# Attention's outputs turned as 4-byte words, and a rearranged start, in a fused attention and MLP kernel

## The chip, the cores and the metric

The kernel runs on one core of a Trainium2 chip. The metric is the device time of one execution in microseconds (us), lower is better. Five engines work side by side, each with its own queue of instructions: PE multiplies matrices (its weight loads are shown apart as PEld), DVE does vector work, ACT evaluates functions and copies, POOL copies, clears and issues DMAs, and SP issues DMAs. Data comes and goes by 16 DMA engines.

## The reference

Local and global attention for 8 batches and 8 heads of 64 dimensions, 512 local and 32 global tokens, and then an MLP with a gated activation over all 4,352 tokens.

```python
s_g = scale * matmul(q_g, k_all^T); out_g = softmax(s_g) @ v_all     # 32 global tokens see all 544
s_ll = where(|i - j| <= 32, scale * matmul(q_l, k_l^T), -1e9)        # 512 local tokens: a band
s_l = concat([scale * matmul(q_l, k_g^T), s_ll])                     # and the 32 global ones
out_l = softmax(s_l) @ concat([v_g, v_l])
x = concat([out_g, out_l]).transpose(0, 2, 1, 3).reshape(4352, 512)
h = x @ w_in                                                         # 512 -> 2048
out = (h * clip(h + 3, 0, 6) / 6) @ w_out                            # 2048 -> 512
```

## The kernel before, in words

**Stages of a batch.** q and k come with tokens on the partitions and are turned by DVE in 32x32 blocks (`turn_words` for batches 0 and 1, in 4-byte words that hold two dimensions of one token; `turn_wide` for the rest). Scores (PE, L712 and L699) go to PSUM. L743 adds the mask and takes the extreme on DVE, L749 is the exponential on ACT, L758 turns the weights of attention on PE, L318 copies them out, L776 sums the values on PE. `normal` divides by the sums (reciprocal L785, product L786) and `xturn` (L799) turns the result on DVE from tokens-by-dimensions to dimensions-by-tokens, into the tile `xt` with four chunks of 128 dimensions. The 32 global tokens go the same way: scores L824 (batches 0 and 1) and L816, value sums L857, product L874, turn L877 into `xg`.

**The MLP.** `first` (L899) multiplies one 128-column tile of w_in with the four chunks of `xt` (L907, 512 columns a matmul; batch 0 comes in parts of 128, 128 and 256 columns), then L918 (relu on ACT, PSUM to `t1`) and L914 (the gate on DVE, to `gts`). `second` (L934) sums 16 chunks of `gts` with w_out, and the result is copied to `ot` and stored. The global tokens of all batches pass through `first` and `second` at the very end.

**The two dimensions of a word.** In `turn_words` q and k are read as words, so that a partition holds two dimensions of each token side by side. The scores of batches 0 and 1 therefore run in two rounds (`bb` 0 and 1), each of which streams every second value (`pairs(kt)[rows, c, ..., bb]`).

**The order of the work.** Every operation is an `Op` with a planned cost per engine, its dependencies and the buffers that it takes, in one of some 35 named streams with a rank each. `Plan.lay` (L122) walks through planned time, and at each step lays the ready operation with the lowest rank on its engine; where an operation may run on several engines, the one that ends it first gets it (DVE with a surcharge `SPARE`). The result is one fixed order per engine. On the chip an engine works through its order and waits for what its data need, whatever the plan thought of the time. The stream names that matter here: `l0` (POOL's loads of the start), `g0` (SP's staging loads of batch 0's q and k), `ga` (ACT's loads of global k and q), `sh` (SP's), `gc`, `gd`, `gp` (casts of global k and q), `msk` (masks), `kg` (halo copies of k, L612), `vs` (strips of v, L542), `tq` (turns of q and k), `nm` and `xp` (`normal` and `xturn`), `t1` and `gate` (L918 and L914).

**The start.** SP loads half of batch 0's q and k as fp32 into the room of w_in (four loads, cast by L431). POOL draws a band for the masks (L385), then issues the other halves of q and k (cast by the DMA), v_g, four pieces of v, four of w_in. `ident` (masks.py) and `clear` (L369, zeroes and ones in the second buffers of `vg`, `kt`, `v0` and `vs`) stand in POOL's order between the first and the second piece of w_in. Batch 1's q follows (to the room of `xt`), k, v, and w_out. `once` (L466) loads global q or k of batch 0 or 1 to 32 partitions in one DMA, and four casts of 32 partitions (L478 on ACT, L480 on DVE or POOL) spread it to four quarters.

Of the kernel before, what the change touches and what calls it, by code (L numbers as in the profile page):

```python
# [37 lines left out]
class Plan:  # L38
# [7 lines left out]
    SPARE, PHASES = 0.5, 9  # L46
# [146 lines left out]
def kernel(  # L193
# [64 lines left out]
    graw0 = tiles("graw0_", 1, [W, 2, H, D], FP32)[0]  # L258
# [37 lines left out]
    for name, rank in (("l0", 0), ("ld", 5), ("lq", -2), ("sh", 0), ("sq", 0), ("st", 3.5), ("g0", 0), ("ga", -9), ("first", -9), ("pad", -30), ("gc", -6), ("gd", 3), ("gp", 3.9), ("cast", -5), ("msk", lambda n: 1 if n < 9 else 1.25), ("tq", lambda n: 0 if n < 8 else 3), ("kg", 0.5), ("vs", 1.5), ("clr", 1),  # L296
                       ("s", 0.5), ("mx", lambda n: 1.2 if n < 33 else 2.7), ("ex", 1.9), ("t", -0.5), ("etc", 0), ("av", -0.7), ("nm", 0.7),
                       ("xp", -0.5), ("gx", 1),
                       ("mf", lambda n: 9 + n * 1e-3), ("ms", lambda n: 9 + (n + len(PARTS) * NDFF + 2) * 1e-3), ("t1", 0), ("gate", -0.7), ("ot", 3)):
        plan.stream(name, rank)  # L300
    for name in ("l0", "ld", "lq", "sh", "st", "g0", "ga", "sq"):
        plan.stream("dq" + name, 0 if name in ("l0", "ld", "lq") else -1)
# [47 lines left out]

    def half(r):

        return slice(r * D, (r + 1) * D)
# [5 lines left out]
    def setup():  # L359
        nc.vector.memset(mxs[0], 0.0)  # L360
        clear(nc.vector, 0)
# [7 lines left out]
    def clear(eng, r):  # L369
        eng.memset(vg[r], 0.0)  # L370
        eng.memset(vg[r][0:W, :, D:D1], 1.0)
        for e in range(2):
# [43 lines left out]

    def stage_loads():
# [3 lines left out]
        there = [[load("g0", "SP", 0.47, 0.65, stage[:, i, c, :], raw(src, 0)[:, c, :], lat=(2.6, 3.1, 3.2, 5.7)[2 * c + i]) for i, src in enumerate((q_l, k_l))]  # L421
# [15 lines left out]
        lower = plan.add("l0", Op(("POOL", 1.9), band))  # L437
        for i, src in enumerate((q_l, k_l)):
            st["qk"][1, i] = [load("l0", "POOL", 0.75, 1.6, nat(0, i)[:, NC // 2:, :], raw(src, 0)[:, NC // 2:, :], lat=4.2 - 0.4 * i)]
        vg_load(0, "l0")  # L440
        for m in (2, 3, NU, 1, 0, NU + 1):
            made["mask", m] = [plan.add("msk", Op(("ACT", 0.21), lambda o=o, i=i: nc.scalar.copy(out=o, in_=i), [lower])) for o, i in places(m)]
# [23 lines left out]
    def once(b, k, src, name):  # L466

        raw_ = (graw0[:, k] if b else ots[k][0:W].rearrange("g (h d) -> g h d", d=D))
        got = load("sh" if b else "ga", "SP" if b else "ACT", 0.47, 0.45 if b else 0.3, raw_, src[b].rearrange("h g d -> g h d"), [w_in_l[1][1]] if b else ())
        g = Buf("gn" + name, 1)  # L470
        state[b]["gn", k] = g
        state[b]["gl"][k] = []
        for e in range(2):
            for f in range(2):
                def cast(engine, e=e, f=f):
                    o, i = gn0[k][quarter(e, f)], raw_.rearrange("g (c e) d -> g e c d", e=2)[:, e]
                    if engine == "ACT":
                        nc.scalar.copy(out=o, in_=i)  # L478
                    else:
                        (nc.gpsimd if engine == "POOL" else nc.vector).tensor_copy(out=o, in_=i)  # L480
                op = Op({"POOL": 0.43, "ACT": 0.42} if b else {"ACT": 0.42, "DVE": 0.4} if k else {"ACT": 0.42}, None, [got], [] if e or f else [g])
                op.emit = lambda op=op, cast=cast: cast(op.engine)
                state[b]["gl"][k].append(plan.add("gp" if b else "gc" if k else "gd", op))
# [33 lines left out]
    def v_loads(b, to):  # L517
# [4 lines left out]
        if b == 0:  # L522
            made["ident"] = plan.add("clr", Op(("POOL", 0.55), lambda: make_identity(nc, ident)))
        vl = [load(to, "POOL", 0.88, 1.05 if b else 1.25, lambda j=j: v0[v.slot][:, j, :, 0:D],
                   v_l[b, :, j * P:(j + 1) * P, :].rearrange("h s d -> s h d"), lat=LATE[b] if b else 3.3 - 0.4 * j) for j in range(NJ)]
# [58 lines left out]
    def turn_words(b, st, k):  # L584
# [23 lines left out]
        def halo(c0, c1, e, engine):  # L608
            copy = nc.scalar.copy if engine == "ACT" else nc.gpsimd.tensor_copy
# [5 lines left out]
        for q in range(n):  # L615
# [10 lines left out]
            else:  # L626
                st["k"].append(plan.add("tq", Op(("DVE", 1.9 / n), lambda c0=c0, c1=c1: turn_q(c0, c1), st["qk"][q, 0],
                                                 [] if b == 0 else [k])))
                a = plan.add("tq", Op(("DVE", 1.95 / n), lambda c0=c0, c1=c1: turn_k(c0, c1), st["qk"][q, 1]))
                st["k"].append(a)  # L630
            for e in range(2):
                h = Op({"POOL": 0.55, "ACT": 0.5}, None, [a])
# [45 lines left out]
    def local(b, n, spare, halves=False):  # L678
# [103 lines left out]
        def normal():  # L782
# [3 lines left out]
            nc.vector.tensor_tensor(out=xs[x.slot].rearrange("p g (a d) -> p g a d", a=2), in0=o[:, :, 0:D].rearrange("p g (d a) -> p g a d", a=2),  # L786
                                    in1=r.rearrange("p g (a d) -> p g a d", a=1).to_broadcast([P, 2 * NC, 2, W]), op=ALU.mult)
# [9 lines left out]
        def xturn():  # L797

            nc.vector.transpose(out=xts[xt.slot][:, :, n * P:(n + 1) * P].rearrange("p k (t q) -> p t k q", q=W),  # L799
                                in_=xs[x.slot].rearrange("p (t k) (a q) -> p t (k a) q", k=2, a=2))  # L800
        st["xT", n] = plan.add("xp", Op(("DVE", 0.7), xturn, done, new, [x]))
# [60 lines left out]
    def globe_values(b):  # L862
# [7 lines left out]
        def normal():  # L870
# [3 lines left out]
            nc.vector.tensor_tensor(out=xgns[xgn.slot].rearrange("p k (a d) -> p k a d", a=2), in0=o[:, :, 0:D].rearrange("p k (d a) -> p k a d", a=2),  # L874
                                    in1=r.rearrange("p k (a d) -> p k a d", a=1).to_broadcast([P, 2, 2, W]), op=ALU.mult)
        n = plan.add("nm", Op(("DVE", 0.45), normal, [a], [rec, xgn], [av, rec]))
        st["xg"] = plan.add("gx", Op(("DVE", 0.22), lambda: nc.vector.transpose(  # L877
            out=xg[:, :, b * Sg:(b + 1) * Sg], in_=xgns[xgn.slot].rearrange("p k (a q) -> p (k a) q", q=W)), [n], (), [xgn]))
# [73 lines left out]
    def moe_first(b):  # L952
# [4 lines left out]
        for at, part in enumerate(PARTS if b == 0 else [range(NJ)]):  # L957
# [3 lines left out]
            for c in range(0, NDFF, per):  # L961
# [6 lines left out]
                got = first(lambda m, cols=cols: xts[xt.slot][:, m, cols], n, cs, gated,  # L968
# [10 lines left out]
    def moe_global():  # L979
        gd, gb = {}, {}  # L980
        deps = [state[b]["xg"] for b in range(B)]
        for c in range(0, NDFF, 2):
# [3 lines left out]
            gd[c] = gd[c + 1] = first(lambda m: xg[:, m, :], B * Sg, range(c, c + 2),  # L986
# [7 lines left out]
    with tc.manual_schedule():  # L994
        clean = plan.add("first", Op(("DVE", 0.1), lambda: nc.vector.memset(zero, 0.0)))
        plan.add("pad", Op(("PE", 4.0), lambda: [nc.tensor.matmul(out=aps[0][0:W, 0, 0:2], lhsT=zero, rhs=zero[:, 0:2], start=True, stop=True) for _ in range(100)], [clean],
# [6 lines left out]
        made["clear"] = plan.add("clr", Op(("POOL", 2.4), lambda: clear(nc.gpsimd, 1), [made["ident"]]))  # L1003
# [76 lines left out]
```

## Time and profile before

| | |
|---|---|
| median of 3 runs | 327.26 us (326.31 to 327.92) |
| profiled execution | 328.56 us, of which the span from the first to the last instruction is 326.8 us |
| granted PE clock | 0.999 |
| L934, second layer, 560 matmuls | 130.8 us busy |
| L907, first layer, 704 matmuls | 121.0 us (640 on `xt`) and 8.9 us (64 on `xg`) |
| L914, gate | 92.1 us on DVE |
| L749, exponential | 84.9 us on ACT |
| L786, product | 32 of 692 ns on DVE |
| L799, turn | 32 of 704 ns on DVE |
| L877, global turn | 8 of 288 ns on DVE |
| L478 and L480, casts of global q and k | 10 of some 400 ns on ACT, 4 of 411 on POOL, 2 of 331 on DVE |

The profile shows one execution. Section 2 of its page cuts the span into 40 slices of 8.17 us, and each digit is the tenths of the slice in which an engine was busy. The chain follows the work back from the last instruction. A row of the windows gives the length of a stretch and each engine's busy time in it, then the PE clock, the DMA engines' mean busy share (over 1 where packets of several queues lie on top of each other) and GB/s. A row of the timeline has start, length, engine, line, operation, output and input, and in brackets how long the engine was idle before it and what ended that. Groups have a count, busy time, mean ns of one and idle time before.

### The profile page before, as it was taken

What the parts mean: (1) busy time and instruction counts of PE and PEld (TensorE: products, weight loads), DVE (VectorE), ACT (ScalarE), POOL (GpSimd) and SP (SyncE); (2) the same over time, 40 slices, a digit from 0 to 9 for tenths busy, and PEclk for the clock granted to TensorE, in tenths of its full rate; (3) what the DMA queues carried; (4) which work ended last, traced back from release to release, by engine and by line L of the source; (5) the groups of instructions that cost most, each with busy time, mean ns of one, the idle gap of its engine ahead of it and who ended that gap; (6) DMA issues with size and microseconds to landing.
All of it is one profiled execution on the core that took longest, in us unless ns stands there. A gap on an engine that the chain in (4) does not pass through costs nothing.

```text
span 326.8 us, 11215 instructions
## 1 busy us (share of the span) xinstructions
PE 305.8 (94%) x4484; PEld 172.8 (53%) x4484; DVE 258.4 (79%) x913; ACT 238.3 (73%) x550; POOL 157.7 (48%) x205
## 2 busy tenths in 40 slices
PE   4477898799999999999999999999999999999995
PEld 4356784454555545555555555555455545556654
DVE  7788996789989897989998999889989985742210
ACT  7999678557895788868876997699759965643221
POOL 9999999029955935665009944963900000000000
PEclk9999999999999999999999999999999999999999
DMA  8999999959952995199949993999111012011223
GB/s 201 180 215 190 188 212 170 230 152 178 200 85 66 140 184 138 46 111 160 217 118 99 226 138 48 148 157 174 33 35 34 2 34 67 0 34 32 65 53 79
DMA packets 104821, 39.54 MB, mean 121 GB/s; under 512 B 91648, under 2 KB 97536, under 8 KB 104768
## 3 DMA queue, kind: packets, MB, share of 16 engines
q0 software_dynamic: 91392, 16.91, 63.9%
q1 hardware_dynamic: 12832, 21.78, 26.8%
q8 instruction: 35, 0.57, 0.7%
q10 hardware_dynamic: 544, 0.13, 0.2%
q14 instruction: 18, 0.15, 0.2%
HBM read 35.13 MB, written 8.91 MB: 135 GB/s over the span
## 4 chain that ended last, share of the span: by engine, by line
PE 86%; POOL 5%; DMA 3%; DVE 2%; issue 2%; ACT 0%; POOLq 0%
PE m L934 37%; PE m L907 35%; PE t L758 4%; DMA xt<-in_q_l_dram 3%; PE a L776 3%; PE s L699 3%; PE t L847 1%; POOL vs L542 1%; PE s L816 1%; POOL v L308 1%; PE a L857 1%; PE s L712 1%; POOL win L308 1%; DVE qt L590 1%; DVE kt L595 1%
## 5 line engine op out<-in xcount | busy, mean ns | idle before, releaser
L934 PE MATMUL m<-wout,gts 128*128 128x512 f16 (+1 forms) x560 | 130.8, 373 | 1.8 <-issue 1.8
L907 PE MATMUL m<-xt,win 128*128 128x512 f16 (+2 forms) x640 | 121.0, 338 | 2.2 <-DVE gts L914 1.2
L914 DVE SCALAR_TENSOR_TENSOR gts<-t,m 128x512 f16<-128x512 f32 x136 | 92.1, 682 | 34.4 <-ACT t L918 33.1
L918 ACT ACTIVATE t<-m 128x512 f32<-128x512 f32 x136 | 81.2, 597 | 34.5 <-PE m L907 31.4
L907 PEld LDWEIGHTS <-win 128*128 128x128 f16 x704 | 70.4, 114 | 48.0 <-issue 3.8
L542 POOL COPY vs<-v 32x1056 f32<-32x1056 f32 (+4 forms) x91 | 81.7, 898 | 29.1 <-DMA v<-in_v_l_dram 24.8
L749 ACT ACTIVATE ex<-sm,mx 128x128 f16<-128x128 f32 x256 | 84.9, 394 | 7.2 <-DVE mx L743 6.5
L934 PEld LDWEIGHTS <-gts 128*128 128x128 f16 x560 | 51.6, 98 | 52.1 <-issue 3.5
L743 DVE CUSTOM_DVE_ANT_0 sm<-s,mask 128x128 f32<-128x128 f32 x240 | 56.2, 285 | 7.2 <-PE s L712 4.1
L308 POOL DMA_DIRECT2D rawq<-in_q_l_dram x12 | 12.6, 1059 | 46.3 <-DVE rec L785 24.3
L318 ACT COPY et<-t 128x1024 f16<-128x1024 f16 x28 | 28.1, 1005 | 8.1 <-PE t L758 8.0
L308 POOL DMA_DIRECT2D v<-in_v_l_dram x32 | 28.2, 896 | 0.0
L942 ACT COPY ot<-m 128x512 f32<-128x512 f32 (+1 forms) x29 | 16.5, 570 | 15.3 <-PE m L934 15.2
L786 DVE TENSOR_TENSOR x<-a,rec 128x512 f16<-128x512 f32 x32 | 22.1, 692 | 1.1
L799 DVE STREAM_TRANSPOSE xt<-x 128x512 f16<-128x512 f16 x32 | 22.5, 704 | 0.1
L758 PEld LDWEIGHTS <-ex 128*128 128x128 f16 x256 | 17.3, 101 | 9.0 <-ACT ex L749 2.7
L743 DVE DVE_READ_ACCUMULATOR2_ANT mx<- 128x1 f32 x256 | 21.3, 83 | 0.0
L758 PE MATMUL t<-ident,ex 128*128 128x128 f16 x240 | 19.9, 225 | 1.5 <-ACT ex L749 1.5
L318 ACT COPY etg<-t 128x640 f16<-128x640 f16 x16 | 11.1, 692 | 10.5 <-PE t L847 10.5
L776 PEld LDWEIGHTS <-et 128*32 128x32 f16 x1024 | 10.0, 98 | 13.1 <-ACT ex L749 4.7
L646 DVE STREAM_TRANSPOSE qt<-rawq 128x512 f16<-128x512 f16 x24 | 15.5, 680 | 0.0
L650 DVE STREAM_TRANSPOSE kt<-rawk 128x512 f16<-128x512 f16 x24 | 15.5, 679 | 0.0
(92 smaller groups left out, 221.5 us busy)
## 6 DMA issues: line engine op xcount, KB each, us to landing
out_dram<-ot SPq DMA_DIRECT2D x62, 128.0 KB, 2.9
vs<-vg SPq DMA_DIRECT2D x32, 132.0 KB, 5.4
v<-in_v_l_dram POOLq DMA_DIRECT2D x32, 128.0 KB, 6.4
rawq<-in_q_l_dram POOLq DMA_DIRECT2D x12, 256.0 KB, 5.8
rawk<-in_k_l_dram POOLq DMA_DIRECT2D x12, 256.0 KB, 6.8
rawq<-rawq SPq DMA_DIRECT2D x12, 254.0 KB, 5.3
rawk<-rawk SPq DMA_DIRECT2D x12, 254.0 KB, 4.9
win<-in_moe_w_in_dram POOLq DMA_DIRECT2D x4, 512.0 KB, 11.3
```

The costliest lines, as they stand in the source:

```text
L308: eng.dma_start(out=o() if callable(o) else o, in_=i() if callable(i) else i)
L318: nc.scalar.copy(out=o(), in_=i())
L542: (nc.gpsimd if op.engine == "POOL" else nc.vector).tensor_copy(out=o(), in_=i())
L743: nc.vector.tensor_tensor_reduce(out=sms[sm.slot], in0=scored(c // 2)[:, z:z + P], in1=mask(m), scale=-scale, scalar=3.0e38, op0=ALU.add, ...
L749: nc.scalar.activation(out=exs[ex.slot][:, un, c, :], in_=sms[sm.slot], func=EXP, scale=-1.0, bias=mxs[mx.slot])
L758: nc.tensor.matmul(out=turned(tp)[:, z:z + P], lhsT=exs[ex.slot][:, un, c, :], rhs=ident, is_transpose=True)
L786: nc.vector.tensor_tensor(out=xs[x.slot].rearrange("p g (a d) -> p g a d", a=2), in0=o[:, :, 0:D].rearrange("p g (d a) -> p g a d", a=2), ...
L799: nc.vector.transpose(out=xts[xt.slot][:, :, n * P:(n + 1) * P].rearrange("p k (t q) -> p t k q", q=W), in_=xs[x.slot].rearrange("p (t k) ...
L907: nc.tensor.matmul(out=mps[ps.slot][:, k * n:(k + 1) * n], lhsT=column_tile(c)[:, m], rhs=x, start=(m == 0), stop=(m == KC - 1))
L914: nc.vector.scalar_tensor_tensor(out=g, in0=shape(t1s[t1.slot][:, 0:all_]), scalar=1.0, in1=shape(mps[ps.slot][:, 0:all_]), op0=ALU.min, o ...
L918: r = plan.add("t1", Op(("ACT", 0.09 + all_ * 0.00083), lambda: nc.scalar.activation(out=t1s[t1.slot][:, 0:all_], in_=mps[ps.slot][:, 0:al ...
L934: nc.tensor.matmul(out=mps[ps.slot][:, 0:n], lhsT=gfn(c), rhs=w_out_t[c // 4][:, c % 4, cols], start=(c == 0), stop=(c == NDFF - 1))
```

## The change

It has five pieces.

1. `normal` writes its product in the order of the dimensions, and `xturn` and the global turn L877 move words of two dimensions, in blocks of 32 words. A partition of `xt` or `xg` then holds two dimensions of a token side by side (`dims`), and L907 streams every second value of it.
2. Global q and k of batches 0 and 1 are loaded straight to the four quarters of 128 partitions, by four DMAs each (batch 0: two of k's by ACT, the other six by SP behind the staging loads; batch 1: eight by SP), and each is cast by one operation on all partitions.
3. POOL's order at the start: band, `ident`, the clear of `vg`, the half loads of q and k, the rest of the clear, v_g, v, w_in. `clear` is cut in two for this.
4. Mask copies may go to DVE as well as ACT, and batch 0's halo copies to DVE as well as POOL and ACT. The turns of batch 1's q and k are four operations each instead of one.
5. Ranks, planned costs and planned landing times of the plan are changed, and with them the order.

The diff, cut to its core:

```diff
-    SPARE, PHASES = 0.5, 9
+    SPARE, PHASES = 0.6, 9
-    graw0 = tiles("graw0_", 1, [W, 2, H, D], FP32)[0]
+    graw0 = tiles("graw0_", 1, [P, 2, NC, D], FP32)[0]
...
-    ("st", 3.5), ... ("tq", lambda n: 0 if n < 8 else 3), ("vs", 1.5), ("nm", 0.7), ("xp", -0.5), ("t1", 0), ("gate", -0.7), ("ot", 3)
+    ("st", 2), ... ("gq", 0.1), ("tq", lambda n: 0.7 if n < 8 else 3.7), ("vs", 3.7), ("nm", 0), ("xp", 1), ("t1", -0.7), ("gate", -1.4), ("ot", 1.5)
...
+    def dims(t):
+        return t.rearrange("p (k a) s -> p k (a s)", a=2).rearrange("p k (s a) -> p k s a", a=2)
...
+    def mask_part(o, i, lower):
+        op = Op({"ACT": 0.18, "DVE": 0.11}, None, [lower])
...
         lower = plan.add("l0", Op(("POOL", 1.9), band))
+        made["ident"] = plan.add("l0", Op(("POOL", 0.55), lambda: make_identity(nc, ident)))
+        plan.add("l0", Op(("POOL", 0.62), lambda: clear_globals(nc.gpsimd, 1)))
         for i, src in enumerate((q_l, k_l)):
-            st["qk"][1, i] = [load("l0", "POOL", 0.75, 1.6, nat(0, i)[:, NC // 2:, :], raw(src, 0)[:, NC // 2:, :], lat=4.2 - 0.4 * i)]
+            st["qk"][1, i] = [load("l0", "POOL", 0.75, 1.6, nat(0, i)[:, NC // 2:, :], raw(src, 0)[:, NC // 2:, :], lat=2.1 - 0.4 * i)]
+        made["clear"] = plan.add("l0", Op(("POOL", 1.9), lambda: clear_rest(nc.gpsimd, 1)))
         vg_load(0, "l0")
...
-        got = load("sh" if b else "ga", "SP" if b else "ACT", 0.47, 0.45 if b else 0.3, raw_, src[b].rearrange("h g d -> g h d"), ...)
-        for e in range(2):
-            for f in range(2):
-                    o, i = gn0[k][quarter(e, f)], raw_.rearrange("g (c e) d -> g e c d", e=2)[:, e]
+        rows = src[b].rearrange("(c e) g d -> e g c d", e=2)
+        for f in range(2):
+            to, engine = ("sh", "SP") if b else ("ga", "ACT") if k and not f else ("gq", "SP")
+            got += [load(to, engine, 0.47, 0.15, raw_[quarter(e, f)], rows[e], ...) for e in range(2)]
+        op = Op({"POOL": 0.43, "ACT": 0.42} if b else {"ACT": 0.42, "DVE": 0.33}, None, got, [g])      # one cast, gn0[k] <- raw_
...
+                pieces = [(c0, c1)] if b == 0 else [(c, c + 1) for c in range(c0, c1)]
+                for x, y in pieces: ... turn_q(x, y)
+                for x, y in pieces: ... turn_k(x, y)
-                h = Op({"POOL": 0.55, "ACT": 0.5}, None, [a])
+                h = Op({"POOL": 0.6, "ACT": 0.5, "DVE": 0.36} if b == 0 else {"POOL": 0.6, "ACT": 0.5}, None, [a])
...
-            nc.vector.tensor_tensor(out=xs[x.slot].rearrange("p g (a d) -> p g a d", a=2), in0=o[:, :, 0:D].rearrange("p g (d a) -> p g a d", a=2), ...)
+            nc.vector.tensor_tensor(out=xs[x.slot], in0=o[:, :, 0:D], in1=r.to_broadcast([P, 2 * NC, D]), op=ALU.mult)
...
-            nc.vector.transpose(out=xts[xt.slot][:, :, n * P:(n + 1) * P].rearrange("p k (t q) -> p t k q", q=W),
-                                in_=xs[x.slot].rearrange("p (t k) (a q) -> p t (k a) q", k=2, a=2))
+            nc.vector.transpose(out=dims(xts[xt.slot])[:, :, n * P:(n + 1) * P, :].rearrange("p k s a -> p k (s a)").bitcast(FP32).rearrange("p k (t q) -> p t k q", q=W),
+                                in_=xs[x.slot].bitcast(FP32).rearrange("p (t k) q -> p t k q", k=2))
...
-                got = first(lambda m, cols=cols: xts[xt.slot][:, m, cols], n, cs, gated,
+                got = first(lambda m, cols=cols: dims(xts[xt.slot])[:, m // 2, cols, m % 2], n, cs, gated,
-            gd[c] = gd[c + 1] = first(lambda m: xg[:, m, :], B * Sg, range(c, c + 2),
+            gd[c] = gd[c + 1] = first(lambda m: dims(xg)[:, m // 2, :, m % 2], B * Sg, range(c, c + 2),
...
-        plan.add("pad", Op(("PE", 4.0), ...))
+        plan.add("pad", Op(("PE", 1.45), ...))
-        made["clear"] = plan.add("clr", Op(("POOL", 2.4), lambda: clear(nc.gpsimd, 1), [made["ident"]]))
```

More of the change, by code (lines that the diff above doesn't have):

```diff
@@ L521, in v_loads @@
         v, strips = st["v"], st["vs"]
[L522 to L525, printed above, removed]
+        vl = [load(to, "POOL", 0.88, 1.05, lambda j=j: v0[v.slot][:, j, :, 0:D],
+                   v_l[b, :, j * P:(j + 1) * P, :].rearrange("h s d -> s h d"), lat=LATE[b] if b else 1.8) for j in range(NJ)]
         def shift(u, z, n, src, js, dj, need):
@@ L608, in halo @@
         def halo(c0, c1, e, engine):
-            copy = nc.scalar.copy if engine == "ACT" else nc.gpsimd.tensor_copy
+            copy = {"ACT": nc.scalar.copy, "POOL": nc.gpsimd.tensor_copy, "DVE": nc.vector.tensor_copy}[engine]
             line = flat(kt[k.slot])
```

70 lines of the change are left out of this document (36 added, 34 removed).

## The prediction

> **What bounds the kernel now.** I read the page first: the busy shares, the 40 slices and the chain.
>
> ```profile
> PE 305.8 (94%) x4484; PEld 172.8 (53%) x4484; DVE 258.4 (79%) x913; ACT 238.3 (73%) x550; POOL 157.7 (48%) x205
> PE   4477898799999999999999999999999999999995
> DVE  7788996789989897989998999889989985742210
> DMA  8999999959952995199949993999111012011223
> PE 86%; POOL 5%; DMA 3%; DVE 2%; issue 2%; ACT 0%; POOLq 0%
> ```
>
> PE is full from the tenth slice on (some 75 us). Before that the slices are not full, and there DMA stands at 9. So the kernel is a start that ends at about 75 us, a PE-bound body, and a tail. The windows put sizes on this.
>
> ```profile
> core 0: us, PE busy (x) PEld busy (x) DVE busy (x) ACT busy (x) POOL busy (x), PEclk, DMA share, GB/s
> 0.00:24.00 24.00, 12.81 (x427) 9.86 (x428) 18.05 (x99) 21.27 (x66) 22.01 (x53) 1.00 1.23 198
> 24.00:50.00 26.00, 22.89 (x509) 19.71 (x507) 24.60 (x75) 21.15 (x50) 24.28 (x34) 1.00 1.45 196
> 50.00:75.00 25.00, 22.23 (x435) 11.64 (x434) 18.74 (x66) 15.87 (x37) 10.42 (x13) 1.00 1.43 180
> 75.00:312.00 237.00, 237.00 (x3054) 125.18 (x3052) 196.20 (x675) 177.24 (x396) 101.02 (x108) 1.00 0.81 102
> ```
>
> In each row: length of the stretch, then PE, PEld, DVE, ACT and POOL busy. Three readings. From 75 to 312 us PE has no idle time, so a faster DVE is worth nothing there. From 24 to 75 us PE idles 3.11 + 2.77 = 5.9 us. Ahead of 24 us ACT (21.27 of 24) and POOL (22.01) are the busy engines, from 24 to 50 us DVE (24.60 of 26). The clock is 1.00 throughout and needs no more thought. Then the timeline, for what starts and holds PE in that stretch.
>
> ```profile
> 8.17 0.70 POOL L308 DMA_DIRECT2D win<-in_moe_w_in_dram  x1
> 12.61 2.14 POOL L308 DMA_DIRECT2D win<-in_moe_w_in_dram  x3
> 24.01 0.47 PEld L907 LDWEIGHTS <-win 128*128 128x128 f16 x4
> 31.08 2.08 DVE L590 STREAM_TRANSPOSE qt<-xt 128x1024 f32<-128x1024 f32 x1
> 37.75 4.69 PE L907 MATMUL m<-xt,win 128*128 128x128 f16 x56 [1.22 <-DVE gts L914]
> 59.09 1.25 PE L934 MATMUL m<-wout,gts 128*128 128x512 f16 x5 [1.85 <-issue]
> ```
>
> The second piece of the first weights is issued at 12.61 us and lands 10.2 us later, at 22.8; the first layer's first matmul is at 24.0. At 31.08 batch 1's q is turned in one block of 2.08 us, and the gates behind it (L914) hold PE: 1.22 us before 37.75. The 1.85 us at 59.09 has no releaser in the profile.
>
> **The change, part by part.**
>
> (1) Word transposes. 32 transposes L799 of 512 half words (704 ns) become 32 of 256 words, 8 of L877 (288 ns) become 8 of 64 words. Word transposes are in the trace:
>
> ```profile
> L799 DVE STREAM_TRANSPOSE xt<-x 128x512 f16<-128x512 f16 x32 | 22.5, 704 | 0.1
> L590 DVE STREAM_TRANSPOSE qt<-xt 128x1024 f32<-128x1024 f32 x1 | 2.1, 2075 | 0.1
> L595 DVE STREAM_TRANSPOSE kt<-wout 128x256 f32<-128x256 f32 x4 | 2.4, 626 | 1.3 <-ACT wout L431 1.2
> L601 DVE STREAM_TRANSPOSE qg<-gn 128x128 f32<-128x128 f32 x2 | 0.6, 302 | 0.3 <-ACT gn L478 0.3
> ```
>
> 128 words take 302 ns and 96 words (L605) 239 ns, so 1.97 ns a word; 256 words come to 302 + 128 x 1.97 = 554 ns, or 626 by L595, whose outputs are scattered. I take 554, since the new outputs lie in runs of 32 words as L601's do: 0.08 to 0.15 us saved each, 2.5 to 4.8 us of DVE in all, and by the same slope 8 x 0.11 = 0.9 us for L877. [...] Of the saving, 24 turns lie beyond 75 us, under a full PE: nothing. Eight lie before, five of them from 24 to 62 us: some 0.6 us.
>
> (2) The normalisation L786 (692 ns) reads the sums in order instead of every second one. The nearest row that reads 512 sums in order is L914's gate with 682 ns: 0 to 0.01 us each, nothing.
>
> (3) The first layer streams every second value: 704 matmuls with 278,528 columns, at 216 ns per 512 in the trace. The scores of batches 0 and 1 stream every second value already. By the starts of single matmuls, eight of L712 (128 columns each) follow each other every 57 ns; contiguous L699's every 55, L907's own 128-column ones every 56. That is 0 to 2 ns per 128 columns, or 0 to 4.4 us over 2,176 such pieces. The other neighbours are the global scores, two rounds of 288 columns: 0.45 us strided (L824) against 0.43 contiguous (L816), by single ends 22 ns per 576 columns, which would be 10.6 us. No row shows a gain, because the contiguous stream is already at its pace. L824 and L712 also load twice the weights for it, which alone can make the difference, so I take 0. [...]
>
> (4) Globals to the quarters. Batch 0 drops six ACT casts (402 ns, L478) and two DVE casts (331 ns) for one whole cast each of q and k; the new one has the same 256 elements per partition, so 0.33 to 0.40 us. ACT saves 1.6 to 2.4 us ahead of 24 us. Batch 1 drops four ACT casts (400) and four POOL ones (411) for two: ACT saves 0.8 to 1.6 us near 30 us. Masks (14 copies, 214 ns) and halo copies may now go to DVE, which has 1.1 to 1.3 us idle in each 5 us from 5 to 20 us. The loads become eight instead of two per batch. Batch 0's six on SP follow the four staging loads (issue 0.4 us each) and end near 5.3 us; SP's next issue is at 10.45. Batch 1's eight take some 4 us of SP, with the next issue at 33.96, so they are covered. What is late next: k's cast now waits for a load issued at 2.6 to 3.5 us, where it was 0.73. ACT's pair landed 3.5 and 4.2 us after issue, so 6.1 to 7.7 us against the first cast at 5.29: up to 2 us later for the first scores (6.78), which the lighter ACT queue gives back by 24 us.
>
> (5) Clearing ahead of loads. On POOL's queue ident (0.5 us) and the clear of vg (0.64) now precede the two half loads (2.52 us), and the rest of the clear (10.07 to 12.66, 2.6 us) precedes vg and the four v loads (4.07). So the half loads go 1.2 us later, v 3.7 later (near 8.4 to 12.0), the first weights at 12.0 instead of 8.17. The other three follow at once and end at 14.9, where they ended at 14.75. The DMA share is 1.23 up to 24 us, so transfer time and not issue set the 22.8. The new order leaves the engines short for about 1.1 us ahead of v and starts POOL's queue 1.2 us late, partly under the staging loads. I take 1.5 us later for the weights and all behind them; bounds 0 (staging gets the engines alone, and fills the gap) and 2.7 (by the packets in the trace, 478 KB of weights are moved by 15 us, at 180 KB/us).
>
> (6) Ranks. The gate (-0.7 to -1.4), the relu (0 to -0.7) and the normalisation (0.7 to 0) go ahead of the turns (0 to 0.7), and batch 1's block of 2.08 us becomes four pieces. This is what acts on the 24 to 50 us stretch: of its 3.1 us of idle I take 2.3 to go. Of the 2.8 us in 50:75, most of it "issue", 1 goes. Planned costs and the changed masks only change the order.
>
> The sum, at the point where PE stays full: -2.3 - 1.0 for idle time, -0.6 for shorter turns, -0.4 for lighter queues ahead of 24 us (more is useless while weights are awaited), +1.5 for the weights: -2.8 us. The profiled execution took 328.56 us (span 326.8 and 1.76 around it), 1.3 over the median 327.26. From 328.56 the sum gives 325.8; on the median's side it is **324.5**. A step of 0.5%, 1.64 us, is what a measurement can tell from none: faster is below 325.6, slower above 328.9.
>
> **Rivals.**
>
> *Weights come later and eat the gain.* For it: DMA is at 9 in nearly every slice up to 65 us, so idle engines are not made up. Against it: the weights' issue ends at the same time. With 2.7 us for 1.5, and 1.5 less idle removed: -2.8 + 1.2 + 1.5, 327.2.
>
> *The strided stream is slower* (the slower side). Place: L907's stream, on the PE-bound path to the end. Price: at L824's pace 10.6 us, 324.5 + 10.6 = 335.1. It makes the kernel slower by over 0.5% from (2.8 + 1.64) / 2,176 = 2.0 ns per 128 columns, 224 ns per 512. For it: L824 against L816. Against it: L712, within 2 ns of the contiguous ones.
>
> *All the idle goes.* If the weights land no later and gates never hold PE, all 5.9 us go: 321.4. Against it: the "issue" gaps belong to no engine that the change speeds up.
>
> *It does not do what it says:* word turns at 0.63 us save half, and the sum is 324.9, inside the forecast.
>
> **Numbers.** Forecast 0.50 (own range 322.5 to 325.6). Weights later 0.25 (326 to 329.5: 0.20 within 0.5%, 0.05 slower). Strided stream 0.10, slower. All idle gone 0.13, faster. Some other lost order 0.02, slower. Faster 0.63, same 0.20, slower 0.17. The range goes from 321.0 to 329.5, which leaves out the strided stream's price, the lost order and a little of each end.
>
> **What would show it.** [...] L907 in 512 columns at 216 ns from start to start; over 221 the gain is gone. The second win piece landing at 24 to 24.5 us. No long transpose block near 31 us and PE's idle time in 24:75 below 3 us. PE still full from 75 to 312 us. I am wrong if the first layer's first matmul is after 26 us, or if PE's body changes its length by more than 2 us.

## The result and the profile after

The changed kernel takes 336.56 us (median of 4 runs, 335.01 to 336.95) against 327.58 (326.31 to 327.92) beside it: ratio 1.0273, 95% interval 1.0229 to 1.0316. It is 9.0 us slower, where 2.8 us less were forecast, and above the range.

The page of the changed kernel, its first lines and its chain of waits (its lines L922, L949, L929, L815, L803, L793 are the L907, L934, L914, L799, L786, L776 of before, with a shift of up to two lines in kernels made from it):

```profile
PE 314.4 (94%) x4484; PEld 176.1 (53%) x4484; DVE 250.8 (75%) x921; ACT 236.7 (71%) x539; POOL 154.9 (46%) x199
PE   3657799999999999999999999999999999999995
DVE  6897696788978798988996998779988855442210
DMA  7999999999962995399739949990111021111222
PE 85%; DMA 8%; DVE 3%; SPq 1%; ACT 1%; issue 0%; ACTq 0%
```

DVE works 7.6 us less and PE 8.6 us more, with the same 4,484 matmuls. In the chain POOL is gone, and DMA has grown from 3 to 8%. The same windows as before, in the changed kernel:

```profile
0.00:24.00 24.00, 12.58 (x420) 9.16 (x420) 19.16 (x97) 16.77 (x49) 21.97 (x52) 1.00 1.14 181
24.00:50.00 26.00, 21.50 (x425) 19.11 (x414) 21.40 (x69) 15.62 (x34) 15.87 (x24) 1.00 1.33 206
50.00:75.00 25.00, 24.63 (x523) 14.37 (x521) 19.32 (x82) 20.69 (x51) 13.92 (x15) 1.00 1.52 169
75.00:312.00 237.00, 236.97 (x3019) 121.96 (x3018) 188.19 (x673) 178.18 (x397) 103.10 (x111) 1.00 0.84 104
```

PE's idle time from 24 to 50 us rose from 3.11 to 4.50, that from 50 to 75 us fell from 2.77 to 0.37, and from 75 to 312 PE is as full as it was: yet it gets through 3,019 matmuls there instead of 3,054. A full engine that gets through less points to a slower engine, which no wait shows; the experiments on the stream test it. ACT is relieved ahead of 24 us (21.27 to 16.77), but the first layer starts no earlier for it. PE's timeline in the changed kernel, where the first layer begins:

```profile
19.97 0.41 PE L793 MATMUL a<-vs,et 128*32 128x65 f16 x16
22.40 0.41 PE L793 MATMUL a<-vs,et 128*32 128x65 f16 x16 [2.02 <-DMA vs<-vg]
24.70 0.41 PE L793 MATMUL a<-vs,et 128*32 128x65 f16 x16 [0.42 <-DVE x L803]
25.87 0.41 PE L793 MATMUL a<-vs,et 128*32 128x65 f16 x16 [0.76 <-DMA vs<-vg]
27.04 2.34 PE L922 MATMUL m<-xt,win 128*128 128x128 f16 x20
42.22 5.03 PE L922 MATMUL m<-xt,win 128*128 128x128 f16 x56 [1.18 <-DVE gts L929]
```

The first layer starts at 27.04 instead of 24.11, and what it waited for is not the weights, but the value sums L793 ahead of it, which wait for the strips of v_g (`vs<-vg`, four DMAs on SP that read `vg`).

The balance, from the starts of PE's instructions in the two profiled executions. Full rate in it is 0.417 ns a column, the slope of contiguous matmuls of 128, 256 and 512 columns, which start every 56, 109 and 216 ns. The last second-layer matmul starts at 330.43 against 322.58, 7.85 us later:

| term | us |
|---|---|
| first matmul of the first layer, 27.04 against 24.11 | +2.93 |
| PE's idle time after it, 3.64 against 5.88 | -2.24 |
| first-layer matmuls, time from one start to the next beyond columns at full rate, 10.04 against 3.72 | +6.32 |
| the rest (attention's matmuls, changes of kind) | +0.84 |

### The profile page after: what moved, and what is told of

It is laid out like the page before. It is cut to its first block, busy times and chain, and to the rows that moved or that the text cites. A ratio compares the mean times of both kernels' runs of the same rounds, so it can differ in the third digit from the quotient of the medians.

```text
span 334.9 us, 11224 instructions
## 1 busy us (share of the span) xinstructions
PE 314.4 (94%) x4484; PEld 176.1 (53%) x4484; DVE 250.8 (75%) x921; ACT 236.7 (71%) x539; POOL 154.9 (46%) x199
## 4 chain that ended last, share of the span: by engine, by line
PE 85%; DMA 8%; DVE 3%; SPq 1%; ACT 1%; issue 0%; ACTq 0%
PE m L949 36%; PE m L922 36%; PE t L775 4%; DMA vs<-vg 4%; PE a L793 3%; DMA graw<-in_q_g_dram 3%; PE s L716 3%; DMA ot<-in_k_g_dram 2%; PE t L863 1%; PE s L832 1%; SPq L308 1%; PE a L873 1%; DVE kt L609 1%; DVE gts L929 1%; PE s L729 1%; DVE qt L604 1%
## 5 line engine op out<-in xcount | busy, mean ns | idle before, releaser
L949 PE MATMUL m<-wout,gts 128*128 128x512 f16 (+1 forms) x560 | 131.8, 373 | 0.0
L922 PE MATMUL m<-xt,win 128*128 128x512 f16 (+2 forms) x640 | 129.5, 349 | 1.2 <-DVE gts L929 1.2
L929 DVE SCALAR_TENSOR_TENSOR gts<-t,m 128x512 f16<-128x512 f32 x136 | 92.6, 684 | 49.6 <-ACT t L933 48.1
L922 PEld LDWEIGHTS <-win 128*128 128x128 f16 x704 | 72.4, 116 | 49.8 <-issue 1.8
L556 POOL COPY vs<-v 32x1056 f32<-32x1056 f32 (+4 forms) x89 | 80.4, 903 | 35.7 <-DMA v<-in_v_l_dram 31.5
L949 PEld LDWEIGHTS <-gts 128*128 128x128 f16 x560 | 51.5, 97 | 51.4 <-issue 1.4
L318 ACT COPY et<-t 128x1024 f16<-128x1024 f16 x30 | 30.2, 1007 | 4.3 <-PE t L775 4.1
L957 ACT COPY ot<-m 128x512 f32<-128x512 f32 (+1 forms) x35 | 20.0, 570 | 17.2 <-PE m L949 17.1
L803 DVE TENSOR_TENSOR x<-a,rec 128x512 f16<-128x512 f32 x32 | 22.1, 692 | 1.1
L775 PE MATMUL t<-ident,ex 128*128 128x128 f16 x248 | 20.9, 227 | 0.4 <-ACT ex L766 0.3
L793 PE MATMUL a<-vs,et 128*32 128x65 f16 x1024 | 14.8, 199 | 4.1 <-DMA vs<-vg 2.8
L793 PEld LDWEIGHTS <-et 128*32 128x32 f16 x1024 | 10.4, 98 | 15.5 <-issue 7.2
L318 ACT COPY etg<-t 128x640 f16<-128x640 f16 x15 | 10.4, 694 | 6.8 <-PE t L863 6.8
```

The source lines that it names most:

```text
L318: nc.scalar.copy(out=o(), in_=i())
L556: (nc.gpsimd if op.engine == "POOL" else nc.vector).tensor_copy(out=o(), in_=i())
L775: nc.tensor.matmul(out=turned(tp)[:, z:z + P], lhsT=exs[ex.slot][:, un, c, :], rhs=ident, is_transpose=True)
L793: nc.tensor.matmul(out=o[hq * W:(hq + 1) * W, 4 * f + 2 * un + kh, 0:D + 1], lhsT=ets[et.slot][:, un, c, quarter(e, f) if b >= WORDS else ...
L803: nc.vector.tensor_tensor(out=xs[x.slot], in0=o[:, :, 0:D], in1=r.to_broadcast([P, 2 * NC, D]), op=ALU.mult)
L922: nc.tensor.matmul(out=mps[ps.slot][:, k * n:(k + 1) * n], lhsT=column_tile(c)[:, m], rhs=x, start=(m == 0), stop=(m == KC - 1))
```

## The experiments

Every run stands beside runs of the kernel before on the same chip (medians 327.3 to 327.9 us). Three theories were put to the test: the strided stream, the rearranged start, and the ranks. The edits of the stream keep the order of every engine. The others change PE's order too, far beyond the start (before_pad_spare only a few rows behind 265 us), so their times hold that as well.

### The stream

*after_halfword_turns* takes piece 1 out of the changed kernel, *before_word_turns* puts piece 1 alone into the kernel before. The order on each engine stays that of the kernel each is made from.

```diff
-            nc.vector.transpose(out=dims(xts[xt.slot])[...].bitcast(FP32)..., in_=xs[x.slot].bitcast(FP32)...)
+            nc.vector.transpose(out=xts[xt.slot][...]..., in_=xs[x.slot].rearrange("p (t k) (a q) -> p t (k a) q", k=2, a=2))
...
-                got = first(lambda m, cols=cols: dims(xts[xt.slot])[:, m // 2, cols, m % 2], n, cs, gated,
+                got = first(lambda m, cols=cols: xts[xt.slot][:, m, cols], n, cs, gated,
```

> The changed kernel with its first piece undone: half-word transposes, contiguous streams of the first layer; order, loads, clears and planned costs as changed. Theory (the strided stream costs 11 ns per 512 columns, 278,528 columns in all, and the moved start costs the rest): 6.0 us less than the changed kernel's 336.6, so 330.6, with the first-layer matmuls of 512 columns at 216 ns from start to start again and its first second-layer matmul still near 53 us. Rival (the new order and start carry the whole loss, the stream is hidden): 336, with the body from 75 us on as long as in the changed kernel.

Measured: 332.34 us, ratio 1.0135 (1.0077 to 1.0194), 4.2 us less than the changed kernel.

> The kernel before with the first piece alone: word transposes and every second value streamed to the first layer; planned costs and so the order of every engine as before. Theory (strided stream, 11 ns per 512 columns): 6.0 us more, less some 0.5 for five shorter transposes ahead of 62 us, 327.3 + 5.5 = 332.8, first-layer matmuls of 512 columns every 227 ns. Rival (the loss is the order and the start): 327, within 0.5% of the kernel before.

(The same lines, the other way round.) Measured: 332.64 us, 1.0147 (1.0092 to 1.0202), 4.9 us more than before. So piece 1 costs 4 to 5 us by itself, taken out or put in, and the rest of the change costs another 4.6 us. In both pairs of profiles the first-layer term of the balance differs by 5.7 us; PE's idle time gives some of it back (4.1 and 0.8 us less with piece 1). To get the law of the stream, batches from the second on were streamed in other steps; these two kernels read other columns of the tile than the layer needs, and serve for the pace alone:

```diff
-                got = first(lambda m, cols=cols: xts[xt.slot][:, m, cols], n, cs, gated,
+                got = first((lambda m: xts[xt.slot].rearrange("p k s -> p (k s)").rearrange("p (s a) -> p s a", a=KC)[:, :, m]) if b else ...)    # before_step4
+                got = first((lambda m: xts[xt.slot].rearrange("p k s -> p (k s)")[:, m:m + 3 * Sl - 2:3]) if b else ...)    # before_step3
```

> The kernel before, in which batches 1 to 7 stream every fourth value of the tile to the first layer instead of consecutive ones (other columns of the same tile, so the products are of other data; batch 0 and the global tokens as before). It measures the pace of a stream by its step: 448 matmuls of 512 columns. If the cost grows with the step (step 2: 11 ns per 512 columns), step 4 gives 230 to 240 ns, 334 to 338 us in all. [...]

> The kernel before, in which batches 1 to 7 stream every third value of the tile to the first layer (other columns of the same tile, so the products are of other data; batch 0 and the global tokens as before). Pace by step so far: 216 ns per 512 columns at step 1, 227 at 2, 454 at 4. [...] If any step but 1 and 2 costs double: 450 ns, 432 us.

Measured: 433.43 us with step 4 and 383.23 with step 3, one execution each. The plainest sight of it is a group of 16 full matmuls of the first layer that follow one another, from the timelines. Contiguous (before):

```profile
143.60 3.62 PE L907 MATMUL m<-xt,win 128*128 128x512 f16 x16
```

Step 2 (before_word_turns), then step 3, then step 4:

```profile
145.48 3.80 PE L909 MATMUL m<-xt,win 128*128 128x512 f16 x16
```

```profile
159.51 5.62 PE L907 MATMUL m<-xt,win 128*128 128x512 f16 x16
```

```profile
174.81 7.43 PE L907 MATMUL m<-xt,win 128*128 128x512 f16 x16
```

The group's length holds 15 steps from start to start and the length of the last matmul, whose mean the groups by shape give. For the contiguous stream, for step 2, for step 3 and for step 4:

```profile
L907 PE MATMUL m<-xt,win 128*128 128x512 f16 x448 | 104.3, 380 | 0.0
```

```profile
L909 PE MATMUL m<-xt,win 128*128 128x512 f16 x448 | 109.0, 389 | 0.0
```

```profile
L907 PE MATMUL m<-xt,win 128*128 128x512 f16 x448 | 160.0, 506 | 0.0
```

```profile
L907 PE MATMUL m<-xt,win 128*128 128x512 f16 x448 | 210.1, 632 | 0.0
L934 PE MATMUL m<-wout,gts 128*128 128x512 f16 x528 | 127.4, 380 | 0.0
```

(3.62 - 0.38) / 15 is 216 ns, (3.80 - 0.39) / 15 is 227, (5.62 - 0.51) / 15 is 341, (7.43 - 0.63) / 15 is 453. Those are 1.00, 1.05, 1.58 and 2.10 of the contiguous pace. The second layer (L934) reads contiguously in all of them and keeps 380 ns, and the other shapes agree: 256 columns take 116 instead of 109 ns, 128 columns 60 instead of 56. The loss doesn't hang on which of the two values is read (medians of 227 to 229 ns for each of the four chunks in the changed kernel), nor on how busy the other engines are: the global tokens' matmuls of 256 columns at the very end, with DVE nearly idle, show it too (116 instead of 109 ns). 11 ns for 512 columns, over 278,528 columns, is 6.0 us, most of the +6.32 of the balance.

### The rearranged start

The loss of 4.6 us that stays in after_halfword_turns was first laid to batch 1's eight loads of global q and k, because ACT waits for them in the changed kernel:

```profile
34.75 0.41 ACT L494 CAST gn<-graw 128x256 f16<-128x256 f32 x1 [3.19 <-DMA graw<-in_q_g_dram]
```

*after_halfword_oldglobals1* is after_halfword_turns with batch 1's global q and k loaded and cast as before, *halfword_oldglobals* with those of both batches, *halfword_oldpool* with POOL's order of the start as before, *halfword_oldpool_oldglobals* with both:

```diff
+    def once(b, k, src, name):
+        (once_spread if b in (1,) else once_quarters)(b, k, src, name)      # (0, 1) in halfword_oldglobals; once_spread is once of before
```

```diff
-        made["ident"] = plan.add("l0", Op(("POOL", 0.55), lambda: make_identity(nc, ident)))
-        plan.add("l0", Op(("POOL", 0.62), lambda: clear_globals(nc.gpsimd, 1)))
...
-        made["clear"] = plan.add("l0", Op(("POOL", 1.9), lambda: clear_rest(nc.gpsimd, 1)))
...
+        made["clear"] = plan.add("clr", Op(("POOL", 2.4), lambda: [clear_globals(nc.gpsimd, 1), clear_rest(nc.gpsimd, 1)], [made["ident"]]))      # halfword_oldpool
```

> The changed kernel with its first piece undone and batch 1's global q and k loaded as before: one load each to 32 partitions and four casts each (batch 0's still by quarters). Theory (the second part of the loss is ACT standing 3.19 us behind batch 1's last global load, which lands at 34.65 us because eight loads are issued on SP, the last at 25.84): 2 to 3 us less than the kernel with the first piece alone undone, about 328. Rival (the start is late because v and its strips come later, whatever the globals do): no less than 330.

Measured: 331.92 us, 1.0124 (1.0072 to 1.0177). Only 0.4 us went: ACT's wait was idle time of an engine that was not the bound, and the theory falls.

> The changed kernel with its first piece undone and POOL's order of the start as before (identity and clear behind the first piece of the weights, v ahead of them), globals by quarters. With the first piece alone undone the kernel took 332.3, 4.6 over the kernel before. Theory (the late v and v_g loads cost it: their strips land at 21.7 us and later and PE waits for them): 329 or less. Rival (the late globals of batch 0 cost it, the first scores start at 8.5 instead of 6.8 us): no less than 331.5. Rival (the new ranks cost it): 332.

Measured: 332.52 us, 1.0142 (1.0115 to 1.0170): no gain.

> The changed kernel with its first piece undone and the globals of both batches loaded as before, POOL's order of the start as changed. Theory (late v): 331.5 or more, as with batch 1's globals alone (331.9). Rival (late globals of batch 0): 329 or less. Rival (ranks): 332.

Measured: 330.84 us, 1.0097 (1.0072 to 1.0122): 1.5 us less than after_halfword_turns, or 1.1 by the distance of each to the kernel before beside it; the two intervals overlap.

> The changed kernel with its first piece undone, POOL's order and all globals as before: what is left of the change is the ranks, the free choice of engine for masks and halo copies, and batch 1's turns in four pieces. Theory (late v): 327 to 328.5. Rival (late globals): the same. Rival (ranks): 331 to 332.

Measured: 331.78 us, 1.0141 (1.0096 to 1.0186). With loads, casts and POOL's order as before, the loss is still there, so what is left must lie in the ranks, in piece 4, or in the order that comes of them.

*halfword_vg_first* tests the wait that the timeline shows: v_g is loaded ahead of the clearing.

```diff
         made["ident"] = plan.add("l0", Op(("POOL", 0.55), lambda: make_identity(nc, ident)))
+        vg_load(0, "l0")
         plan.add("l0", Op(("POOL", 0.62), lambda: clear_globals(nc.gpsimd, 1)))
...
-        vg_load(0, "l0")
```

> The changed kernel with its first piece undone, and batch 0's v_g loaded first of POOL's loads, ahead of the clear of vg and the half loads (its buffer is cleared by DVE). With the first piece alone undone it took 332.3; there and in the changed kernel PE waits for the strips of v_g that SP copies (landing at up to 25.8 us), and the first layer starts at 25.9 and 27.0 instead of 24.1. Theory (the late strips of v_g set the start): they land before 20 us, the first layer starts near 24, 329.5 to 330.5. Rival (v's own strips and the weights are late as well, and the strips of v_g only came last): first layer near 25.5, 331.5 or more.

Measured: 330.38 us, 1.0077 (1.0045 to 1.0108). The strips land by 17.4 us instead of 24.7 (25.8 in the changed kernel), the waits for them are gone, and 2.0 us with them. The first layer nevertheless starts at 26.07, since the next wait is behind DVE (L841 is the scores of the global tokens):

```profile
19.49 0.63 PE L793 MATMUL a<-vs,et 128*32 128x65 f16 x32 [1.08 <-ACT et L318]
23.78 0.68 PE L841 MATMUL s<-kt,qg 32*32 32x288 f16 x16 [2.03 <-DVE mx L760]
26.07 1.49 PE L924 MATMUL m<-xt,win 128*128 128x128 f16 x12
```

### The ranks

*before_new_ranks* gives the kernel before all new ranks, with `SPARE` and the planned cost of `pad`; *halfword_old_ranks* gives after_halfword_turns the old ones.

```diff
-    SPARE, PHASES = 0.5, 9
+    SPARE, PHASES = 0.6, 9
...
-    ("st", 3.5), ("tq", lambda n: 0 if n < 8 else 3), ("vs", 1.5), ("nm", 0.7), ("xp", -0.5), ("t1", 0), ("gate", -0.7), ("ot", 3)
+    ("st", 2), ("tq", lambda n: 0.7 if n < 8 else 3.7), ("vs", 3.7), ("nm", 0), ("xp", 1), ("t1", -0.7), ("gate", -1.4), ("ot", 1.5)
```

> The kernel before with the new ranks, surcharge and planned cost of the first matmuls alone. Theory (late v and late globals): 326 to 328, no loss. Rival (ranks): 331 to 332.

Measured: 331.44 us, 1.0147 (1.0085 to 1.0209). The ranks alone, with no other part of the change, cost 4 us.

> The changed kernel with its first piece undone and with the old ranks, surcharge and planned cost of the first matmuls: what is left of the change is globals by quarters, POOL's order of the start, masks and halo copies on more engines, batch 1's turns in four pieces. With the first piece alone undone it took 332.3; the new ranks alone cost 4.1 on the kernel before. Theory (the ranks carry the second loss): 327 to 329. Rival (the moved start costs as much by itself, and the ranks only where the start is old): 331 to 333.

Measured: 333.38 us, 1.0173 (1.0140 to 1.0205). With old ranks the moved start (with piece 4) loses 5.8 us instead of 4.6; the intervals overlap. The two losses don't add up: each is there without the other, and both together are not larger.

Then the ranks by groups: *before_ranks_dve* (tq, nm, xp, t1, gate), *before_ranks_strips* (vs, st, ot), *before_pad_spare* (`pad` and `SPARE`), and one by one *before_strip_rank_only* (vs 1.5 to 3.7) and *before_copy_rank_only* (ot 3 to 1.5).

> The kernel before with the new ranks of the turns of q and k, normalisation, turn of the outputs, relu and gate alone. The order of the instructions shows what they do: relu's and gate's ranks by themselves change no row on any engine, normalisation's and the output turn's 11 rows on DVE, and the turns' rank the rest (batches 1 and later). Theory (turns of q and k laid later hold up the scores): 329 to 331. Rival (strips' rank): 327.

Measured: 328.41 us, 1.0032 (1.0007 to 1.0057).

> The kernel before with the new planned cost of the first 100 matmuls (4.0 to 1.45) and DVE's new surcharge (0.5 to 0.6) alone. Both other theories: 327, within 0.5%. Rival (PE's order is laid by a plan that now starts 2.5 us sooner and meets its fetches of instructions elsewhere): 329 to 331.

Measured: 328.04 us, 1.0020 (0.9982 to 1.0057), not to be told from none.

> The kernel before with the new ranks of v's strips (1.5 to 3.7), of the stores (3.5 to 2) and of the output copies (3 to 1.5) alone. Theory (turns' rank): 327. Rival (strips laid later hold up the value sums, or the copies press on ACT and DVE): 329 to 331.

Measured: 332.14 us, 1.0120 (1.0078 to 1.0161).

> The kernel before with the new rank of v's strips alone (1.5 to 3.7). Strips, stores and copies together took 332.1. Theory (POOL's strips behind other work hold up the value sums): 331 to 332. Rival (the output copies): 327 to 328.

Measured: 332.11 us, 1.0124 (1.0077 to 1.0170).

> The kernel before with the new rank of the output copies alone (3 to 1.5; the stores' rank changes nothing beside it in PE's, ACT's, POOL's or SP's order). Theory (strips): 327 to 328. Rival (copies go ahead of the exponentials on ACT or of the gates on DVE): 330 to 332.

Measured: 330.06 us, 1.0062 (1.0034 to 1.0089).

The rank of the strips of v (the stream `vs` holds those of every batch) costs as much as all ranks together. The gate's and the relu's ranks, on which the forecast had built much of its gain, by themselves change no row of any engine's order in the kernel before. What the strips' rank does in batch 0 is seen in the groups of `vs<-v` up to 32 us. On DVE, in the kernel before and then in before_strip_rank_only:

```profile
L542 DVE COPY vs<-v 32x264 f32<-32x264 f32 x3 | 1.2, 405 | 0.1
```

```profile
L542 DVE COPY vs<-v 32x264 f32<-32x264 f32 (+1 forms) x8 | 3.5, 437 | 0.2
```

The plan lays the strips later, finds ACT taken, and gives eight to DVE instead of three (ten in the changed kernel, 4.8 us); and PE waits behind DVE (before_strip_rank_only):

```profile
22.73 0.68 PE L824 MATMUL s<-kt,qg 32*32 32x288 f16 x16 [1.02 <-DVE mx L743]
39.74 2.82 PE L907 MATMUL m<-xt,win 128*128 128x128 f16 x40 [1.48 <-DVE gts L914]
```

That made a good story, and the last two runs tested it, by taking DVE out of the strips' engines: *strip_rank_no_dve* with the new rank on the kernel before, *halfword_vg_no_dve* on halfword_vg_first.

```diff
-        op = Op({"POOL": 0.25 + 0.205 * len(js), "ACT": 0.2 + 0.22 * len(js), "DVE": c if n == W else 1.35 * c} if b == 0 else {"POOL": c}, ...)
+        op = Op({"POOL": 0.25 + 0.205 * len(js), "ACT": 0.2 + 0.22 * len(js)} if b == 0 else {"POOL": c}, ...)
```

> The kernel before with the rank of batch 0's strips of v at 3.7 instead of 1.5 (as in the run with that rank alone, 332.1 us, ratio 1.0124), and DVE taken out of the engines that may copy them. In the planned order DVE then copies none (8 with the rank alone, 3 in the kernel before), ACT 2 pieces, POOL the rest. Theory 'strips on DVE hold the gates': the loss goes, 327 to 329 us, ratio below 1.006, and PE's idle time from 18 to 40 us goes back from 7.6 to some 5 us. Rival 'the strips come too late, whoever copies them': 331 to 333 us, and PE idles in front of the value sums L776 instead of behind the gates.

Measured: 332.58 us, 1.0111 (1.0041 to 1.0180). DVE copies no strip, the first layer starts at 24.05, as early as in the kernel before, and nothing is gained. The wait behind the gates even grows:

```profile
39.01 4.45 PE L907 MATMUL m<-xt,win 128*128 128x128 f16 x40 [2.21 <-DVE gts L914]
```

So the theory falls: the rank's loss doesn't come from who copies the strips. PE's order, though, is row for row that of before_strip_rank_only. The rival that the strips come too late for the value sums isn't borne out either, since the value sums L776 wait some 0.6 us longer in all (1.07, 0.55 and 0.30 us against 1.08 and 0.19).

> The changed kernel without the word turns (contiguous stream), with v_g loaded ahead of the clearing (that run took 330.4 us, ratio 1.0077), and DVE taken out of the engines that may copy batch 0's strips: 10 pieces go from DVE to POOL and ACT. Theory 'strips on DVE hold the gates': some 2 us less than 330.4, 328 to 329 us, not below the kernel before since the weights still land 1 to 3 us later. Rival 'the rest of the loss is the later weights and loads of v alone': 330 to 331.5 us, unchanged.

Measured: 330.76 us, 1.0079 (1.0042 to 1.0116), as without this edit (330.38), although the first layer now starts at 23.56. No version beat the kernel before.

## Why the prediction was wrong, step by step

**Step 3, the strided stream, taken at 0, is the step that failed.** It is worth +6.3 us in the balance, and 4.2 to 4.9 us by the runs that take piece 1 out or put it in alone. The rival had the right mechanism and place, and its point of decision (224 ns per 512 columns) was passed by 3 ns; its price of 10.6 us was 1.7 times too high. That its 335.1 us lies near the measured 336.56 is luck, since the time also holds 4.6 us of the start and the ranks, which the rival doesn't have. L712's bound (0 to 4.4 us) was too low, L824's (10.6) too high, and the choice between them wrong: the pair L824 against L816 showed a cost, it was put down to the doubled weight loads, and the lowest end was taken for the whole. Step 2 measured 1.05 times the contiguous pace (227 against 216 ns per 512 columns), step 3 1.58 (341) and step 4 2.10 (453).

**Step 5, clearing ahead of loads, was right on the weights and missed their neighbour.** The second piece of the first weights landed at 23.99 us (24 to 24.5 forecast). But the first layer's first matmul came at 27.04, 2.9 us later where 1.5 were forecast, and beyond the 26 that the text had named as proof against it. The load of v_g was moved behind the clearing too; SP's four strips, which copy from it, followed (issued from 11.62 instead of 10.45) and came into the thick of the other loads: the last landed at 25.8 instead of 22.6. The step counted the loads that POOL issues, and not the DMA of another queue that waits for one of them. With v_g first, 2.0 us come back.

**Step 6, the ranks: the mechanism was wrong, and the idle time that went is in part luck.** Of the 5.88 us of PE's idle time from 24 to 75 us, 3.3 were to go; 1.0 went. From 24 to 50 us, where the ranks were to act, it rose by 1.4. Counted from the first layer's start it fell by 2.24, but 3.4 of the 5.88 are gaps without a releaser (0.67, 0.92 and 1.85 us), and these come and go: before_pad_spare, with PE's order of the kernel before up to 265 us, lacks two of them, and idles 3.88 us from 24 to 75. The gate's and relu's ranks reorder nothing. In after_halfword_turns, with the same order and a contiguous stream, the idle time is 7.78 us and not 3.64: with piece 1 idle time goes down, which fits a slower PE that waits less for the same gates, though no run took that alone, and in before_word_turns it goes down by 0.8 us only. And the strips' rank, which the text passed over among the ones that "only change the order", costs 4.4 us by itself.

**Step 1, word transposes, was sized too dear.** The turns in the changed kernel:

```profile
L815 DVE STREAM_TRANSPOSE xt<-x 128x256 f32<-128x256 f32 x32 | 14.0, 436 | 0.2
L892 DVE STREAM_TRANSPOSE xg<-xgn 128x64 f32<-128x64 f32 x8 | 1.9, 235 | 0.1
```

436 ns, not 554: each saves 268 ns, some 8.6 us of DVE in all. From 128 words (302 ns in L601 of before, 286 in the same row of the changed kernel) to 256 a word costs 1.05 to 1.17 ns; the text took 1.97, the slope from 96 to 128 words. Most of DVE's saving lies under a full PE, as the text said; no run has the turns without the stream, so what the rest is worth is not shown.

**Steps 2 and 4.** The product L803 stayed at 692 ns, as forecast. k's cast came later, as forecast: the first scores are at 9.02 instead of 6.78, and ACT's lighter queue didn't give that back: with the globals loaded as before, 1.1 to 1.5 us were gained (halfword_oldglobals), within the intervals of the two runs.

**What stays open.** Why the rank of the strips costs 4.4 us in the kernel before, and why the moved start and the ranks each cost 4 to 6 us but not their sum, is not settled, and piece 4 was never run alone. In strip_rank_no_dve's profiled execution the loss of 5.1 us at the last second-layer start splits into 0.8 of idle time, about 1.7 from a lower clock (below) and 2.6 in the matmuls of the first layer and of attention (the second layer loses none); but executions of these kernels at a granted clock of 1.00 lose some 4 us as well, and none of those was profiled.

The traces point to a rival that no run tested: PE's own order. The strips' rank changes it throughout. Behind 75 us PE goes 108 times from a matmul on the whole array to one on a part of it, or back, in both runs that have that rank alone; the kernel before does so 90 times, and after_halfword_turns, which has the rank too but another start, 86 times. By an estimate from the starts of PE's matmuls, with each kind at its mean pace in the kernel before, the two runs lose some 2.5 us behind 75 us, before_copy_rank_only (102 changes) 1.5, before_ranks_dve (100) 1.0, before_pad_spare (90) nothing, and after_halfword_turns 1.2, of which 1.0 is idle time. That the changes themselves cost this is not shown.

## What to carry to other kernels

Where PE is the bound, as it is here from 75 to 312 us, weigh the layout that PE streams against what it saves on the engine that writes it: 5% on the moving operand (227 against 216 ns) cost more than a third off every transpose (436 against 704 ns) could give back, by 4 to 5 us. When bounds for an unshown cost are far apart and the path to the end runs through it, take the row that shows a cost, or measure that one row first. When a load moves, follow what reads its target on every other queue, and expect any rank to reorder operations that it doesn't name.

## What the runs showed of the hardware

**The pace of a strided moving operand.** For 512 columns of fp16 values: 216 ns contiguous, 227 in steps of two values, 341 of three, 453 of four. From two to four it is proportional to the step, 113 to 114 ns for each value of it. A contiguous stream would take 113 ns by that (an estimate from these three) and took 216. What in the stride sets the pace is not shown.

**The clock fell after some gaps of about 2 us, and not after others.** PE's granted clock was expected to be 1.00 throughout. In halfword_vg_no_dve PE is idle for 1.88 us, and then:

```profile
27.58 0.26 PE L924 MATMUL m<-xt,win 128*128 128x128 f16 x1 [1.88 <-issue]
```

```profile
25.00:27.00 2.00, 0.70 (x11) 0.59 (x11) 1.83 (x5) 2.00 (x7) 1.86 (x4) 1.00 1.14 206
27.00:28.00 1.00, 0.42 (x5) 0.42 (x5) 0.00 (x0) 1.00 (x5) 0.94 (x2) 0.81 1.15 206
28.00:31.00 3.00, 3.00 (x67) 2.25 (x65) 2.03 (x4) 2.94 (x7) 2.90 (x6) 0.50 1.21 204
31.00:32.00 1.00, 0.67 (x37) 0.44 (x35) 0.91 (x3) 1.00 (x3) 1.00 (x2) 0.98 1.25 214
```

The third column from the end is the clock: 0.50 for the 3 us of the third row (3.41 us in the clock's own record), in which PE is full at about half the pace (8 matmuls L924 from 30.30 take 0.97 us, where 11 from 24.89 took 0.81): by an estimate from the clock 1.5 us lost and 0.2 around it, almost as much as the gap. A gap of 1.92 us in before_strip_rank_only was followed by the same from 54 to 57 us (0.50), and that execution took 333.70 against 331.79 and 331.86 of two at clock 1.00. In strip_rank_no_dve the clock was 0.55 from 39 to 42 us and 0.82 from 42 to 44, behind the wait of 2.21 us before 39.01. The kernel before has a gap of 1.85 us at 59 and keeps its clock, and so do before_word_turns with one of 2.39 us at 59 and before_ranks_strips with one of 2.68 us at 57; so gaps of this size stand with a dip behind them and without one, and that the gap sets it off is not shown.

**PE's gaps without a releaser stand at fixed places of its order.** In all profiles together PE has 33 such gaps of over 0.6 us behind 24 us. 32 of them come just before the 479th or 480th, the 606th, the 989th or 990th, the 1118th or the 1245th matmul: places that lie 128 matmuls apart, or a multiple of it, to within two, which is 256 instructions with the weight load of each. Whether a gap is there, and its length (0.62 to 2.68 us), differs from profile to profile. The kernel's plan reckons with a fetch after every 256 instructions of PE (`BLOCK`); that fetches are the cause is not shown.
